# P times V in two row halves of the array: 64-key halves, two PSUM banks, a GpSimd sum, and scores one slot later

## The chip, the cores and the metric

The kernel runs on one core of a Trainium2 chip. The metric is the device time of one execution in microseconds (us). Before the change it is 1067.9 us, the median of three runs (1067.76 to 1069.48).

## What is computed

A block with attention and a gated feed-forward layer side by side, in fp32, on 2048 tokens of width 640:

```python
def _A_ref(x, wqkv, wo):
    H = 32; Dh = D // H; W = 256
    # q, k, v = x @ wqkv, split into 32 heads of 20
    scores = jnp.einsum("bhqd,bhkd->bhqk", q, k) * (Dh ** -0.5)
    mask = (idx[:, None] - idx[None, :] >= 0) & (idx[:, None] - idx[None, :] < W)
    p = _softmax(jnp.where(mask[None, None], scores, -1e9), axis=-1)
    o = jnp.einsum("bhqk,bhkd->bhqd", p, v)
    return o.reshape(B, S, D) @ wo

def _B_ref(x, w_gate, w_up, w_down):
    return (_gelu(x @ w_gate) * (x @ w_up)) @ w_down

xn = _layernorm(A_x)
return A_x + _A_ref(xn, A_wqkv, A_wo) + _B_ref(xn, B_w_gate, B_w_up, B_w_down)
```

What matters here is the window: a query attends to itself and to the 255 keys before it. So a block of 128 keys is seen by 128 + 256 = 384 consecutive queries, and a half block of 64 keys by 64 + 256 = 320.

## The kernel before

The attention is worked off in 32 units `u`: 8 groups `g` of four heads times 4 chunks `c` of 512 queries. A unit is 14 slots long (`NS`), and the loop in `attention()` writes out by hand, slot by slot, the order of TensorE (PE), ScalarE (ACT), VectorE (DVE) and GpSimd (POOL). A slot holds, in this order: the actions that earlier code put off to it (`defer`, `late`, kept by `at` and `tick`), some max work, the scores, and about three (`RATE / NS`) filler matmuls on TensorE (`pull_fill`, line 105): the projections of later heads and part of the feed-forward layer, which would have to be done anyway. After the last unit the rest of the filler runs, and then the remaining feed-forward layer and the output products (lines 901 and 1168).

What is done for a unit, in time order:

- `max_pair` (matmuls on line 473, the reduction on line 477): a first product of scores in bf16 whose row maximum DVE takes. The two heads of a pair stand in the two row halves of the array, each with a PSUM bank of its own from the pool `psm`.
- `exp_piece` (matmuls on line 532, exponential on line 534): the scores again, transposed so that keys lie on the partitions and queries along the free axis, for one head and one of three groups of key blocks X, Z, Y (`pieces`), then ACT writes `exp` into the tile P (`pts[u, bi]`, 128 keys by 4 heads by 512, three buffers). Two pieces are done in each of the even slots 0 to 10. The scores stand in the PSUM pool `psx`, which has two banks.
- `clear` (lines 545 and 548): POOL sets the P entries outside the window to zero, one slot after the last head of a group.
- `av_unit` (line 559), in slot 0 of the next unit: P times V. For each key block of the unit the 128 keys are the contraction, and the four heads stand in four column strips of 32 of the array, with 20 columns of V and a column of ones (the softmax denominator) each. The result of all key blocks is summed in one PSUM bank `ps_o`, from the same pool `psx`. Chunks c > 0 have six key blocks d = -2 to 3 relative to the chunk's first, seen by 128, 256, 384, 384, 256 and 128 of the chunk's 512 queries; chunk 0 has the four blocks d = 0 to 3. ACT then copies the bank to `ob` (line 563), and three slots later `store` issues five DMAs on the SyncE queue (SP): four heads, and the denominators (lines 567 and 568).

P and V are fp32, for which a matmul of the program is executed as two records of a weight load and a matmul: 24 units of 6 blocks and 8 of 4, with 4 heads, are 704 products, and the trace has 1408 records on line 559. Line 105 has single records on hi and lo parts of its operands (fp32r), lines 473 and 532 are bf16.

`load_stack` fetches the scores' operands for unit u + 3 in slots 9 and 12 over SP.

Of the kernel before, what the change touches and what calls it, by code (L numbers as in the profile page):

```python
# [19 lines left out]
C = 512  # L20
# [45 lines left out]
def block_kernel(ctx, tc, x, wqk, wv, wgu, wdo, wdl, out):  # L66
    nc = tc.nc
# [65 lines left out]
    psx = pp.enter_context(tc.tile_pool(name="psx", bufs=2, space=PSUM))  # L133
# [61 lines left out]
    def at(slot, fn, *a):  # L195
        acts.setdefault(slot, []).append((fn, a))
# [9 lines left out]
    def flush():  # L206
        while lates:
            fn, a = lates.pop(0)
            fn(*a)
# [108 lines left out]
    def run(*gens):  # L318
        for gen in gens:
            for _ in gen:  # L320
                pass
# [118 lines left out]
    vtiles = dict(enumerate(v0[2]))  # L440
    ap = pr.enter_context(tc.tile_pool(name="ap", bufs=2, side="right", reuse_waits="tile"))

    def load_stack(u, which=(0, 1)):
        g, c = divmod(u, NC)
        for m in range(80 * g // 128, (80 * g + 79) // 128 + 1):
            assert all((m + 5 * i, c) in done for i in which), (u, m)

        for i in which:
            dst, src, top, again = ((qs[u % NQ], qd[c], 1, 2), (ks[u % NK], kd[c], 0, 0))[i]
            for j in (0, 2):  # L450
                for p, part, n in ((j * 32, top, 2), (j * 32 + 2 * DH, again, 1), (64 - j * 32, 0, 3)):
                    nc.sync.dma_start(dst[p:p + DH * n, j:j + 2].rearrange("p j t -> p (j t)"),
                                      src[g, part:part + n].rearrange("s (d j) t -> (s d) (j t)",
                                                                      j=4)[:, j * C:(j + 2) * C])
# [44 lines left out]
    def pieces(c):  # L499
        b = 4 * c  # L500
        X = [(b, 0, 0, 384)] + ([(b - 2, 384, 0, 128)] if c else [])
        Y = [(b + 1, 0, 128, 384), (b + 3, 384, 384, 128)]
        Z = ([(b - 1, 0, 0, 256)] if c else []) + [(b + 2, 256, 256, 256)]
        return X, Z, Y
# [11 lines left out]
    pts = {}  # L516

    def exp_piece(u, s):
        g, c = divmod(u, NC)
        bi, j = divmod(s, 4)  # L520
        bank = pieces(c)[bi]
        q = qs[u % NQ]
        if j == 0:
            pts[u, bi] = ap.tile([128, 4, C], F32, name="P", tag="P", bufs=3)
        pt = pts[u, bi]
        lo = min(p[1] for p in bank)
        hi = max(p[1] + p[3] for p in bank)
        ps = psx.tile([128, C], F32, name="ps_e", tag="ex")
        for kb, col, q0, n in sorted(bank, key=lambda p: p[3]):
            k = ks[(u - (kb < 4 * c)) % NK]  # L530
            kc = kb % 4 * 128
            nc.tensor.matmul(ps[:, col:col + n], k[0:QROWS, j, kc:kc + 128], q[0:QROWS, j, q0:q0 + n],  # L532
                             start=True, stop=True)
        nc.scalar.activation(pt[:, j, lo:hi], ps[:, lo:hi], AF.Exp, scale=SCALE)  # L534
        if j == 3:
            defer(1, clear, u, bi)
# [13 lines left out]

    def av_unit(u):
        g, c = divmod(u, NC)
        o, v = psx.tile([128, C], F32, name="ps_o", tag="ex"), vtiles[g]
        todo = [(pts[u, bi], *p) for bi, bank in enumerate(pieces(c)) for p in bank]
        for i, (pt, kb, col, q0, n) in enumerate(todo):
            assert (id(v), kb) in done, (u, kb)
            for j in range(4):
                w0_ = kb * 84 + 21 * j
                nc.tensor.matmul(o[32 * j:32 * j + 32, q0:q0 + n], v[:, w0_:w0_ + 32], pt[:, j, col:col + n],  # L559
                                 start=i == 0, stop=i == len(todo) - 1, skip_group_check=True,  # L560
                                 tile_position=(0, 32 * j))
        ob = ap.tile([128, C], F32, name="ob", tag="ob", bufs=1)
        nc.scalar.activation(ob, o, AF.Copy)  # L563

        def store():
            for j in range(4):
                nc.sync.dma_start(od[c].rearrange("(d h) t -> h d t", h=H)[4 * g + j], ob[32 * j:32 * j + DH, :])
            nc.sync.dma_start(sd[c][4 * g:4 * g + 4, :], ob[DH::32, :])

        defer(3, store)  # L570

    def load_gu(f):
        raws = []
# [105 lines left out]
    def x_sums(p, k, half):  # L679
        w = C // 2  # L680
        a, b = (slice((2 * p + i) * C + half * w, (2 * p + i) * C + half * w + w) for i in (0, 1))
        eh, el = xh.bitcast(F32), xl.bitcast(F32)
        live = {}

        def tile_of(i):
            live[i] = ap.tile([128, w], F32, name="tx", tag="tx")
            return live[i]

        def pool(o, i, j, op):
            nc.gpsimd.tensor_tensor(out=o, in0=i, in1=j, op=op)  # L690

        def store(i):
            t = live[i]
            defer(2, lambda: nc.sync.dma_start(td[p][i][:, k, half * w:half * w + w], t))

        def s1():
            pool(tile_of(1), eh[:, k, b], eh[:, k, a], OP.subtract)

        def s2():
            pool(live[1], live[1], el[:, k, b], OP.add)  # L700

        def s3():
# [12 lines left out]

        def s7():
            pool(live[4], live[4], el[:, k + 2, a], OP.add)
            store(4)

        def s8():  # L720
            pool(tile_of(3), eh[:, k + 2, b], eh[:, k, b], OP.subtract)

        def s9():
            pool(live[3], live[3], el[:, k + 2, b], OP.add)

        def s10():
# [28 lines left out]
    def attention():  # L755
        now[0] = -1
        load_stack(0)
        load_stack(1)
        load_stack(2)
        for i, (p, k, half) in enumerate((p, k, half) for p in range(NC // 2) for k in range(2) for half in range(2)):  # L760
            for j, fn in enumerate(x_sums(p, k, half)):
                at(XS0 + XSN * i + 2 * j, fn)
        for i in range(12):
            now[0] = i - 13
            for fn, a in tick():
                fn(*a)
            if i % 2 == 0:
                pull_max(2, now[0])
            flush()
            pull_fill(2 * RAMP)  # L770
        pull_fill(GAP)
        for u in range(NU + 1):
            for i in range(NS):
                T = now[0] = NS * u + i
                for fn, a in tick():
                    fn(*a)
                if i in (0, 4, 8) or T == 2:
                    pull_max(2, T)
                if i == 0 and u:
                    av_unit(u - 1)  # L780
                    flush()
                    pull_max(2, T)
                if i % 2 == 0 and i < 12 and u < NU:
                    exp_piece(u, i)
                    if i == 0 and u:
                        pull_fill(1)
                        debt[0] -= 1
                    exp_piece(u, i + 1)
                flush()
                if u + 3 < NU and i in (KSLOT, 12):  # L790
                    load_stack(u + 3, (int(i == KSLOT),))
                pull_fill(RATE / NS)
        while acts:
            now[0] += 1
            for fn, a in tick():
                fn(*a)
            flush()
        now[0] = None
        run(fill)
        assert not acts  # L800
# [82 lines left out]
    def gate_up_pair(f, w, p, extra, keep=False):  # L883
# [51 lines left out]
        for h, i, g, c in ((h2, qp, g2, 2 * p + 1), (h1, u1, g1, 2 * p)):  # L935
# [3 lines left out]
            else:  # L939
# [4 lines left out]
    place = {("b", 0): "xh1", ("b", 1): "xl1", ("b", 2): "xh0", ("b", 3): "xl0",  # L944
             ("t", 0): "xh2", ("t", 1): "xl2", ("t", 2): "xh3", ("t", 8): "xl3"}
# [433 lines left out]
    for n, (p, k) in enumerate(steps):  # L1379
        i = n % (NQD + 1)  # L1380
# [71 lines left out]
```

## Time and profile before

| | us |
|---|---|
| median of three runs | 1067.9 |
| span of the profiled execution | 1070.0 |
| TensorE busy | 1055.2 |
| VectorE busy | 746.0 |
| ScalarE busy | 518.8 |
| GpSimd busy | 337.8 |
| P times V on TensorE (line 559), 32 units | 84.3 |

The profile is one execution. "PE" is TensorE's matmuls and "PEld" its weight loads, which run beside them. A row of the page's groups reads: line, engine, operation, out<-in, shapes, count, then the busy time and the mean of one, then the idle time of the engine just before it and what ended most of it. A row of the timeline reads: start, length, engine, line, operation, tiles, shape, count; neighbouring instructions of one line are merged into a row, whose shape is that of the first. Ends of matmuls are modelled, so starts are the better guide.

### The profile page before, as it was taken

Reading aid. Unit: us, or ns where it says so; the run is one execution under the profiler, and the core shown is the slowest. Engines: PE = TensorE matmul, PEld = TensorE weight load, DVE = VectorE, ACT = ScalarE, POOL = GpSimd, SP = SyncE. Lnnn points to the kernel's source line nnn. Section 1 sums busy time; section 2 is a strip of 40 time slices with the busy share of each in tenths; the row PEclk is TensorE's granted clock in tenths of the full one; section 3 lists DMA queues with packets and bytes.
Section 4 is the critical chain, followed back from the end, with each engine's and each line's share of the span. In section 5 each row is a group of like instructions: output and inputs, shape, how many; then the busy total and the mean of one; then the engine's idle time right before and its main releaser. Section 6 shows DMA issues by size and latency. Waiting matters only on the chain.

```text
span 1070.0 us, 21147 instructions
## 1 busy us (share of the span) xinstructions
PE 1055.2 (99%) x7253; PEld 830.4 (78%) x7253; DVE 746.0 (70%) x1985; ACT 518.8 (48%) x1088; POOL 337.8 (32%) x514
## 2 busy tenths in 40 slices
PE   8999999999999999999999999999999999999998
PEld 8877666666677766666666668888888999999998
DVE  7845667665565566776767716787776879888887
ACT  4434565566556565565556565332234544433332
POOL 5021564767554383736346340211100000000000
PEclk9999999999999999999999999999999999999999
DMA  5642344446452244424334116576677873443443
GB/s 196 189 131 85 114 135 126 145 131 187 131 153 86 86 120 139 150 85 134 96 116 130 55 60 198 172 245 207 244 247 240 274 261 120 129 131 109 132 132 104
DMA packets 105172, 158.46 MB, mean 148 GB/s; under 512 B 15420, under 2 KB 60092, under 8 KB 105064
## 3 DMA queue, kind: packets, MB, share of 16 engines
q1 hardware_dynamic: 102680, 150.95, 44.5%
q10 hardware_dynamic: 2384, 6.16, 1.8%
q8 instruction: 57, 0.93, 0.4%
q14 instruction: 51, 0.42, 0.1%
HBM read 101.78 MB, written 54.92 MB: 146 GB/s over the span
## 4 chain that ended last, share of the span: by engine, by line
PE 86%; DVE 7%; DMA 2%; ACT 2%; issue 2%; POOL 1%; SPq 0%; ACTq 0%; DVEq 0%; POOLq 0%
PE ps_d L105 27%; PE ps L1168 16%; PE ps_g L901 15%; PE ps_e L532 8%; PE ps_o L559 6%; PE ps_v L105 6%; PE ps_m L473 5%; DVE junk L477 2%; PE ps_g L105 1%; DMA hr<-hd 1%; DVE ss L1006 1%; PE ps_t L180 1%; DVE wt L1006 1%; DVE at L1006 1%; ACT wb L987 1%
## 5 line engine op out<-in xcount | busy, mean ns | idle before, releaser
L477 DVE CUSTOM_DVE_ANT_0 junk<-ps_m,mask 128x384 bf16<-128x384 f32 (+2 forms) x512 | 272.6, 532 | 150.5 <-PE ps_m L473 92.7
L534 ACT ACTIVATE P<-ps_e 128x512 f32<-128x512 f32 (+2 forms) x384 | 198.5, 569 | 93.6 <-PE ps_e L532 79.9
L1168 PE MATMUL ps<-wb,at 128*128 128x320 f32 x999 | 156.7, 309 | 1.1 <-DVE xr L1191 0.7
L1168 PEld LDWEIGHTS ps<-wb,at 128*128 128x128 f32 x999 | 148.9, 188 | 2.1 <-issue 0.9
L545 POOL TENSOR_SCALAR_AFFINE_SELECT P<-P 128x512 f32<-128x512 f32 x128 | 86.1, 672 | 168.0 <-ACT P L534 165.7
L105 PE MATMUL ps_d<-xh,wql 128*128 128x512 f32 x430 | 130.5, 415 | 0.0
L105 PE MATMUL ps_d<-xh,wqh 128*128 128x512 f32 x430 | 129.2, 413 | 0.0
L105 PE MATMUL ps_d<-xl,wqh 128*128 128x512 f32 x430 | 129.2, 412 | 0.0
L532 PE MATMUL ps_e<-qs,ks 124*128 124x128 bf16 (+2 forms) x704 | 117.7, 279 | 0.2 <-ACT ob L563 0.2
L532 PEld LDWEIGHTS <-ks 124*128 124x128 bf16 x704 | 49.6, 98 | 60.5 <-issue 51.1
L105 PEld LDWEIGHTS ps_d<-xl,wqh 128*128 128x128 f32 x430 | 80.1, 191 | 14.8 <-issue 0.8
L105 PEld LDWEIGHTS ps_d<-xh,wql 128*128 128x128 f32 x430 | 80.0, 191 | 13.8
L105 PEld LDWEIGHTS ps_d<-xh,wqh 128*128 128x128 f32 x430 | 79.1, 189 | 15.0 <-ACT xh L188 1.4
L1168 PE MATMUL ps<-wt,at 128*128 128x320 f32 x552 | 89.2, 310 | 0.8 <-DVE xr L1191 0.8
L559 PE MATMUL ps_o<-P,v 128*32 128x384 f32 (+2 forms) x1408 | 84.3, 386 | 0.0
L1168 PEld LDWEIGHTS ps<-wt,at 128*128 128x128 f32 x552 | 82.9, 188 | 1.3 <-DVE xr L1191 1.0
L548 POOL TENSOR_SCALAR_AFFINE_SELECT P<-P 128x512 f32<-128x512 f32 x112 | 72.9, 661 | 28.7 <-ACT P L534 28.7
L1122 ACT ACTIVATE at<-ss 128x512 fp32r<-128x512 f32 x59 | 37.3, 632 | 88.3 <-DVE ss L1006 88.3
L244 POOL TENSOR_TENSOR pt<-r,pt 128x512 bf16<-128x512 f32 x40 | 46.6, 1164 | 90.7 <-ACT pt L243 76.9
L559 PEld LDWEIGHTS ps_o<-P,v 128*32 128x32 f32 x1408 | 41.4, 110 | 39.7 <-issue 25.1
L473 PE MATMUL ps_m<-ks,qs 60*128 60x128 bf16 (+1 forms) x704 | 67.0, 275 | 4.8 <-DVE mx L477 3.1
L563 ACT ACTIVATE ob<-ps_o 128x512 f32<-128x512 f32 x32 | 19.1, 597 | 93.2 <-PE ps_o L559 80.1
(189 smaller groups left out, 1682.4 us busy)
## 6 DMA issues: line engine op xcount, KB each, us to landing
hr<-hd SPq DMA_DIRECT2D x104, 128.0 KB
hd<-he SPq DMA_DIRECT2D x50, 256.0 KB
wr<-wgu SPq DMA_DIRECT2D x27, 320.0 KB
qs<-qd SPq DMA_DIRECT2D x64, 120.0 KB
ks<-kd SPq DMA_DIRECT2D x64, 120.0 KB
xi<-x SPq DMA_DIRECT2D x16, 320.0 KB
qs<-qd SPq DMA_DIRECT2D x64, 80.0 KB
ks<-kd SPq DMA_DIRECT2D x64, 80.0 KB
```

The costliest lines, as they stand in the source:

```text
L105: nc.tensor.matmul(ps, a(k), b(k), start=n == 0, stop=n == 3 * nk - 1)
L244: nc.gpsimd.tensor_tensor(out=pt[:, l, :], in0=r, in1=pt[:, 1, :], op=OP.subtract)
L473: nc.tensor.matmul(ps[:, lo:hi], q[rows, j, 128 * b:128 * b + 128], kt[rows, j, k0:k1], start=True, stop=True, tile_position=(64 * r, 0))
L477: nc.vector.tensor_tensor_reduce(out=junk[:, 0:n], in0=ps[:, 0:n], in1=mask[:, 384 - n:384], scale=1.0, scalar=NEG, op0=OP.add, op1=OP.max ...
L532: nc.tensor.matmul(ps[:, col:col + n], k[0:QROWS, j, kc:kc + 128], q[0:QROWS, j, q0:q0 + n], start=True, stop=True)
L534: nc.scalar.activation(pt[:, j, lo:hi], ps[:, lo:hi], AF.Exp, scale=SCALE)
L545: nc.gpsimd.affine_select(out=a, in_=a, pattern=[[0, 4], [1, 128]], compare_op=OP.is_ge, fill=0.0, base=0, channel_multiplier=-1)
L548: nc.gpsimd.affine_select(out=a, in_=a, pattern=[[0, 4], [-1, 128]], compare_op=OP.is_ge, fill=0.0, base=-1, channel_multiplier=1)
L559: nc.tensor.matmul(o[32 * j:32 * j + 32, q0:q0 + n], v[:, w0_:w0_ + 32], pt[:, j, col:col + n], start=i == 0, stop=i == len(todo) - 1, ski ...
L901: nc.tensor.matmul(ps, i, j, start=first and n == 0, stop=n == len(work) - 1, skip_group_check=True)
L1122: nc.scalar.activation(hi[:, 3:7], s, AF.Copy)
L1168: nc.tensor.matmul(ps[bank][:, 0:HD], *work[bank][j], start=bank not in begun, stop=final[p, bank] == n and j == len(work[bank]) - 1, skip ...
```

## The change

Each key block is taken as two halves r = 0, 1 of 64 keys. The half with r = 0 (partitions 0 to 63 of V and P) stands in the upper row half of the array, the half with r = 1 in the lower one, so a product has 64 rows and 32 columns, at one of eight positions. A half is multiplied with its 320 queries only, cut to the chunk. Each row half sums into a PSUM bank of its own, both from `psx`. The order of the halves is written out (`steps_`): six pairs, one of each row half, with 320, 256, 192, 320, 128 and 64 queries for c > 0; in chunk 0 the halves that belong to blocks before the sequence are left out.

ACT copies the first bank to `ob` and the second to a part of the P tile of group Y, which is read no more (`oc`). Three slots later POOL adds the two (`join`), and the store is put off from three slots to five. The scores' pieces stand in the odd slots 1 to 11 in place of the even ones, with the same two pieces in each.

```diff
     def av_unit(u):
         g, c = divmod(u, NC)
-        o, v = psx.tile([128, C], F32, name="ps_o", tag="ex"), vtiles[g]
-        todo = [(pts[u, bi], *p) for bi, bank in enumerate(pieces(c)) for p in bank]
-        for i, (pt, kb, col, q0, n) in enumerate(todo):
+        v = vtiles[g]
+        os = [psx.tile([128, C], F32, name="ps_o", tag="ex") for _ in range(2)]
+        place = {kb - 4 * c: (pts[u, bi], col, q0) for bi, bank in enumerate(pieces(c)) for kb, col, q0, n in bank}
+
+        def half(d, r):
+            i = 2 * d + r
+            return d, r, max(0, 64 * i), min(C, 64 * i + 320)
+
+        steps_ = [((0, 0), (0, 1)), ((2, 0), (-1, 1)), ((-1, 0), (2, 1)), ((1, 0), (1, 1)),
+                  ((3, 0), (-2, 1)), ((-2, 0), (3, 1))]
+        todo = [half(*x) for pair in steps_ for x in pair if x[0] in place]
+        begun_, left = set(), [sum(t[1] == r for t in todo) for r in range(2)]
+        for d, r, qa, qb in todo:
+            pt, col, q0 = place[d]
+            kb = 4 * c + d
...
+            rows = slice(64 * r, 64 * r + 64)
             for j in range(4):
                 w0_ = kb * 84 + 21 * j
-                nc.tensor.matmul(o[32 * j:32 * j + 32, q0:q0 + n], v[:, w0_:w0_ + 32], pt[:, j, col:col + n],
-                                 start=i == 0, stop=i == len(todo) - 1, skip_group_check=True,
-                                 tile_position=(0, 32 * j))
-        ob = ap.tile([128, C], F32, name="ob", tag="ob", bufs=1)
-        nc.scalar.activation(ob, o, AF.Copy)
+                nc.tensor.matmul(os[r][32 * j:32 * j + 32, qa:qb], v[rows, w0_:w0_ + 32],
+                                 pt[rows, j, col + qa - q0:col + qb - q0], start=r not in begun_,
+                                 stop=not left[r], skip_group_check=True, tile_position=(64 * r, 32 * j))
+            begun_.add(r)
+        ob, oc = ap.tile([128, C], F32, name="ob", tag="ob", bufs=1), pts[u, 2][:, 0]
+        lo = 0 if c else 64
+        nc.scalar.activation(ob, os[0], AF.Copy)
+        nc.scalar.activation(oc[:, lo:], os[1][:, lo:], AF.Copy)
+
+        def join():
+            nc.gpsimd.tensor_tensor(out=ob[:, lo:], in0=ob[:, lo:], in1=oc[:, lo:], op=OP.add)
...
-        defer(3, store)
+        defer(3, join)
+        defer(5, store)
...
-                if i % 2 == 0 and i < 12 and u < NU:
-                    exp_piece(u, i)
-                    if i == 0 and u:
+                if i % 2 and i < 12 and u < NU:
+                    exp_piece(u, i - 1)
+                    if i == 1 and u:
                         pull_fill(1)
                         debt[0] -= 1
-                    exp_piece(u, i + 1)
+                    exp_piece(u, i)
```

More of the change, by code (lines that the diff above doesn't have):

```diff
@@ L552, in av_unit @@
         g, c = divmod(u, NC)
-        o, v = psx.tile([128, C], F32, name="ps_o", tag="ex"), vtiles[g]
-        todo = [(pts[u, bi], *p) for bi, bank in enumerate(pieces(c)) for p in bank]
-        for i, (pt, kb, col, q0, n) in enumerate(todo):
+        v = vtiles[g]
[11 more added lines that the diff above has]
+            kb = 4 * c + d
             assert (id(v), kb) in done, (u, kb)
+            left[r] -= 1
+            rows = slice(64 * r, 64 * r + 64)
             for j in range(4):
                 w0_ = kb * 84 + 21 * j
-                nc.tensor.matmul(o[32 * j:32 * j + 32, q0:q0 + n], v[:, w0_:w0_ + 32], pt[:, j, col:col + n],
-                                 start=i == 0, stop=i == len(todo) - 1, skip_group_check=True,
-                                 tile_position=(0, 32 * j))
-        ob = ap.tile([128, C], F32, name="ob", tag="ob", bufs=1)
-        nc.scalar.activation(ob, o, AF.Copy)
+                nc.tensor.matmul(os[r][32 * j:32 * j + 32, qa:qb], v[rows, w0_:w0_ + 32],
[8 more added lines that the diff above has]
+            nc.gpsimd.tensor_tensor(out=ob[:, lo:], in0=ob[:, lo:], in1=oc[:, lo:], op=OP.add)
         def store():
```

## The prediction

> **What bounds the kernel now.** I read the page's busy times and slices first, then the chain that ended last, then busy times by stage, and last who waited for whom.
>
> ```profile
> span 1070.0 us, 21147 instructions
> PE 1055.2 (99%) x7253; PEld 830.4 (78%) x7253; DVE 746.0 (70%) x1985; ACT 518.8 (48%) x1088; POOL 337.8 (32%) x514
> PE   8999999999999999999999999999999999999998
> PE 86%; DVE 7%; DMA 2%; ACT 2%; issue 2%; POOL 1%; SPq 0%; ACTq 0%; DVEq 0%; POOLq 0%
> ```
> ```profile
> 110.00:640.00 530.00, 526.80 (x4163) 351.65 (x4166) 333.07 (x1104) 308.19 (x654) 287.69 (x454) 1.00 0.40 119
> ```
> ```profile
> PE ps_m L473 <- DVE mx L477: 3.1, 9, 0.5
> PE ps_e L532 <- ACT ob L563: 0.2, 1, 0.2
> ```
>
> In the stage with attention (110 to 640 us; columns PE, PEld, DVE, ACT, POOL, granted clock, DMA share, GB/s) TensorE is busy for 526.8 of 530 us at full clock, the others at most 333. TensorE's waits there are 3.1 us for the row maxima and 0.2 for the copy of P times V. So what a matmul costs is paid in full, and work on the others is free as long as nobody on TensorE waits for it. The filler is a fixed amount: time saved in a unit ends the stage earlier.
>
> P times V, by unit: two calls of the windows view restricted to line 559, one over the 8 units of chunk 0 and one over the 24 others; the first row and the sum of each.
>
> ```profile
> 110.30:113.60 3.30, 2.15 (x32) 0.94 (x32) 1.00 0.00 0
> sum 26.40, PE 17.17 PEld 7.46; mean PE 2.15 PEld 0.93
> ```
> ```profile
> 127.30:130.60 3.30, 2.80 (x48) 1.42 (x48) 1.00 0.49 147
> sum 79.20, PE 67.14 PEld 33.98; mean PE 2.80 PEld 1.42
> ```
>
> Chunk 0 streams 384 + 384 + 256 + 128 = 1152 queries per head, the others 1536. Then 67.14 / 24 - 17.17 / 8 = 0.651 us for 384 queries: **1.70 ns per query**, all four heads and both records together.
>
> How the array is shared shows in one unit's timeline.
>
> ```profile
> 400.57 1.30 PE L105 MATMUL ps_d<-xh,wqh 128*128 128x512 f32 x5
> 401.70 0.84 PE L105 MATMUL ps_d<-xh,wql 128*128 128x512 f32 x3
> 401.95 0.63 POOL L545 TENSOR_SCALAR_AFFINE_SELECT P<-P 128x512 f32<-128x512 f32 x1
> 402.91 0.16 PEld L559 LDWEIGHTS ps_o<-P,v 128*32 128x32 f32 x8 [0.16 <-issue]
> 402.91 2.80 PE L559 MATMUL ps_o<-P,v 128*32 128x384 f32 x48
> 403.26 0.13 PEld L559 LDWEIGHTS ps_o<-P,v 128*32 128x32 f32 x4 [0.19 <-issue]
> 403.58 1.21 PEld L559 LDWEIGHTS ps_o<-P,v 128*32 128x32 f32 x28 [0.19 <-issue]
> ...
> 405.64 0.50 PE L473 MATMUL ps_m<-ks,qs 60*128 60x384 bf16 x4
> 405.78 0.60 ACT L563 ACTIVATE ob<-ps_o 128x512 f32<-128x512 f32 x1 [2.37 <-DMA qs<-qd]
> 406.07 0.39 PE L532 MATMUL ps_e<-qs,ks 124*128 124x128 bf16 x2
> ```
>
> A plain matmul of 512 columns takes (401.70 - 400.57) / 5 = 0.226 us, 0.44 ns per column. The weight loads of P times V come in fours, 403.58 - 403.26 = 0.32 us apart for 384 queries: 0.84 ns per query for a round of four records, about twice a plain pass. So a round is the four column strips at work together, and a block is two rounds. Two row halves work together too, in line 473: four matmuls of 384 columns take 406.07 - 405.64 = 0.43 us with the switch at their end, where one after the other they would take 4 x 384 x 0.44 ns = 0.68 us. No row shows four strips and two row halves at once, and that is what the change stands on.
>
> **The change, part by part.**
>
> *Fewer queries per array position.* A row half streams 320 + 256 + 192 + 320 + 128 + 64 = 1280 queries in place of 1536; in chunk 0, 1024 (upper) and 896 (lower) in place of 1152. If all eight positions work at once, a unit saves 256 x 1.70 ns = 0.435 us, in chunk 0 128 x 1.70 = 0.217 us: 24 x 0.435 + 8 x 0.217 = **-12.2 us**. Its bounds are the rivals below: from this to a sum in which the halves do not overlap.
>
> *Twice the weight loads and matmuls*: 1408 more of each.
>
> ```profile
> L559 PEld LDWEIGHTS ps_o<-P,v x1408: 105/110/110, 110.4 to 640.3; 128*32 128x32 f32 x176
> L559 PE MATMUL ps_o<-P,v x1408: 272/379/511, 110.4 to 640.4; 128*32 128x384 f32 x64, 128*32 128x256 f32 x56, 128*32 128x128 f32 x56
> L559 PEldq EVENT_SEMAPHORE  x31: 51/51/51, 107.8 to 636.0; - x31
> ```
>
> A load (0.110 us) runs behind the round before it. A round of 64 queries lasts 64 x 0.84 = 0.054 us, so the last two of a unit can each be 0.056 us late: at most 32 x 0.112 = +3.6 us, at best 0, since loads and matmuls start together at 402.91. I take +1.0, nearer that row.
> Feeding them: eight loads start within 0.16 - 0.11 = 0.05 us at 402.91, 6 ns each, and the sequencer passes the first unit's semaphore at 107.8, 2.6 us ahead of the first matmul (110.4). So I cost it at nothing; the upper bound is the pace of line 473, 0.43 us for four records, 0.11 us each, and is a rival.
> The Trainium skill ("TensorE: Matmul & The Clock Gate", "Wait — 56ns, not 53.3ns?") gives a floor of about 25 ns from start to start. By it 96 matmuls would take at least 2.4 us, an estimate, a unit would save 0.2 us in place of 0.435, and the time would come out near 1063; the 6 ns above disagree for different array positions.
>
> *A second bank, a second copy.* Both banks of `psx` are taken by P times V, whose first matmul so waits for both last exponentials; these lie two slots back. After it ACT makes two copies. Before, the copy starts 405.78 - 405.64 = 0.14 us after the next matmul and takes 0.60; so `ob` is done 0.74 and `oc` at most 1.34 us after that matmul. In the built order four of line 473 (0.43) and three of line 105 (0.68) come before the first scores: 1.11 us. One more of line 105 and the first scores (512 columns each, 0.45) come before the second: 1.56 us. Both are covered, the second by 0.2 us. Without the filler the second scores would wait 1.34 - 0.43 - 0.23 = 0.68 us, 32 x 0.68 = +22 us. I take +0.5. ACT's 32 x 0.60 = 19 us lie in 530 - 308 us of room.
>
> *The sum on POOL.*
>
> ```profile
> L244 POOL TENSOR_TENSOR pt<-r,pt 128x512 bf16<-128x512 f32 x40 | 46.6, 1164 | 90.7 <-ACT pt L243 76.9
> L545 POOL TENSOR_SCALAR_AFFINE_SELECT P<-P 128x512 f32<-128x512 f32 x128 | 86.1, 672 | 168.0 <-ACT P L534 165.7
> ```
> ```profile
> L559 PE MATMUL ps_o<-P,v 128*32 128x384 f32 (+2 forms) x1408 | 84.3, 386 | 0.0
> ```
> ```profile
>   PEld ps_o L559: 2.0, 11
> ```
>
> An add of this size takes 1.164 us (line 244): 32 x 1.164 = 37 us on POOL, 288 + 37 = 325 of 530. It stands in slot 3, when both copies have long landed. Behind it on POOL are the clears of the new unit's X, not read before the next P times V ten slots on, and the lo parts of filler weights. Cost 0. The five store DMAs move two slots back on SP, behind other stores but ahead of the loads of slot 9, which serve three units later; `ob` is written again 14 slots on. Cost 0.
>
> *Scores one slot later.* In the built order three fewer matmuls of line 105 lie between the last scores and P times V: the last clear ends 0.68 us later, at 402.58 + 0.68 = 403.26 in this unit, 0.35 us after the start at 402.91. Group Y is first needed after 320 + 256 + 192 queries, 1.30 us in. Line 545 lists 2.0 us in 11 waits of weight loads for POOL; the matmuls of line 559 have no idle time before them. I take +0.3; a unit in four late by 0.4 us would be +3.
>
> Sum on the profiled time: 1070.0 - 12.2 + 1.0 + 0.5 + 0.3 = 1059.6. The median of the runs lies 2.1 us below the span: **1057.5 us, rounded to 1057**.
>
> **The rivals.**
>
> *A: order is kept between the row halves of a strip.* The program issues, for each half, a head's two records one behind the other. If the lower half's first record does not pass the upper half's second, only neighbours overlap. Rounds of a unit are then 320, then each pair's own length (1280 in sum), the larger of neighbouring pairs (320 + 256 + 320 + 320 + 128), and 64: 3008 queries at 0.85 ns, against 2 x 1536 = 3072. That is -0.054 us per unit, in chunk 0 2368 against 2304 or +0.054: -0.9 us in all, +1.8 from above: 1070.9 on the profiled time, 1068.8 on the median. For it: line 473 alternates halves with one record each, so no row shows a passing. Against it: in the strips the four heads do work together although each has two records to do.
> The Trainium skill (same page, Part 3, "The mechanism") says that matmuls start and end in strict program order. By that rule this rival is what happens; the loads in fours agree with it only if the order is not head by head.
>
> *B, the other side: the array takes four streams at a time.* Place: the 24 + 8 blocks of line 559. Price: the halves run one after the other, 2560 queries against 1536 and in chunk 0 1920 against 1152: 24 x 1024 x 1.70 ns + 8 x 768 x 1.70 = 41.8 + 10.4 = +52 us, 1120 on the median. It decides as soon as rounds hold four records instead of eight (break-even is at 4 x 2560 / 1536 = 6.7). For it: every round in the trace has four. Against it: line 473 reads two row halves at once, and the data per partition and time are the same as before.
>
> *C: feeding binds.* At 0.11 us per record 96 take 10.6 us; at half that, with the queue filled ahead, 5.3 us: (5.3 - 2.8) x 24 + (3.5 - 2.15) x 8 = +71, 1139. Against it: the lead of 2.6 us.
>
> *D: a new wait.* The cover after P times V is too short because ACT comes late to the copies, and half of the 22 us above is paid: 1057 + 11 = 1068; all of it, 1079.
>
> **How the numbers follow.** Forecast 0.55, A 0.17, B 0.10, C 0.05, D 0.13. About 0.2% (2.1 us) is what a measurement of this kernel can tell from no change. Faster takes the forecast and a sliver of D: 0.56. Same takes most of A and a part of D: 0.16. Slower is B, C, the rest of D and a bit of A: 0.28. The forecast's own range is 1055 (no cost at all, 1067.9 - 12.2) to 1063 (3.6 for loads, 3 for clears). To hold 8 in 10 it is carried over A and D to 1079, with 1054 below; B and C are left out.
>
> **What would show each step.** Forecast: loads of P times V in eights, a unit of about 2.37 us busy (chunk 0: 1.94), line 559's successor at about 72 us in all, and still about 0 idle before the scores. A: 2.75 us per unit, loads in fours. B: 4.5 us. C: rounds further apart than 0.84 ns per query, with "issue" as what ended the gaps. D: idle time of the scores' matmuls with the copies as releaser, or of P times V with POOL. The forecast is wrong if the unit does not shrink, or if it does and TensorE's idle time in the stage grows by more than 4 us.

## The result and the profile after

| | before | after |
|---|---|---|
| median of the runs, us | 1068.69 (4 runs, 1067.76 to 1070.49) | 1077.11 (4 runs, 1075.19 to 1078.79) |
| span of the profiled execution, us | 1070.0 | 1073.8 |
| P times V on TensorE, us | 84.3 | 76.2 |

The changed kernel is slower by 0.75%: ratio 1.0075, 95% interval 1.0056 to 1.0094. Forecast were 1057 us and "faster"; 1077 lies inside the stated range only because that range was carried over rivals A and D, and neither of them came true. Part of the scatter of the runs goes with the granted clock of a run: those of before that were taken with experiments 1 to 4 took 1066.0 to 1068.2 us at 1.0 and 1070.9 to 1071.7 at 0.995. From the profile's page of the changed kernel, the busy times and the chain:

```profile
span 1073.8 us, 24088 instructions
...
PE 1056.4 (98%) x8661; PEld 824.3 (77%) x8661; DVE 753.1 (70%) x1985; ACT 531.4 (49%) x1120; POOL 373.8 (35%) x546
...
PE 81%; DVE 6%; DMA 4%; POOL 3%; issue 3%; ACT 2%; SPq 1%; ACTq 0%; DVEq 0%; POOLq 0%
```

TensorE still is the bound. But it is busy for 1.2 us more than before although P times V takes 8.1 us less. The groups by line, for P times V and for the filler:

```profile
L105 PE MATMUL ps_d<-xh,wql 128*128 128x512 f32 x430 | 136.8, 421 | 0.0
L573 PE MATMUL ps_o<-P,v 64*32 64x320 f32 (+4 forms) x2816 | 76.2, 348 | 2.5 <-ACT P L534 1.8 <-POOL P L548 0.5
L105 PEld LDWEIGHTS ps_d<-xl,wqh 128*128 128x128 f32 x430 | 77.4, 189 | 18.6 <-issue 7.6
L105 PEld LDWEIGHTS ps_d<-xh,wql 128*128 128x128 f32 x430 | 77.0, 189 | 20.7 <-issue 10.2
L105 PEld LDWEIGHTS ps_d<-xh,wqh 128*128 128x128 f32 x430 | 76.7, 189 | 21.1 <-issue 8.9 <-ACT xh L188 1.4 <-DVE he L648 0.3
```

The same groups before:

```profile
L105 PE MATMUL ps_d<-xh,wql 128*128 128x512 f32 x430 | 130.5, 415 | 0.0
L105 PEld LDWEIGHTS ps_d<-xl,wqh 128*128 128x128 f32 x430 | 80.1, 191 | 14.8 <-issue 0.8
L105 PEld LDWEIGHTS ps_d<-xh,wql 128*128 128x128 f32 x430 | 80.0, 191 | 13.8
```

Two things stand out. The filler, in which not one instruction was changed, got dearer: 136.8 for 130.5 us in one of its three groups. And its weight loads now stand idle for 7 to 10 us per group with "issue" as the releaser, where it was 0.8 or nothing. "Issue" names no tile; the timeline has to say where it is. P times V has idle time of its own, 2.5 us, mostly on the last exponentials.

To see where the stage gained and lost, every TensorE matmul between the first and the last P times V was charged from its own start to the start of the next, and the times were added by kind of work. "Places" counts how often TensorE comes into the filler from maximum work or from the small matmul that transposes the maxima (line 494), and not from scores. Times in us:

```
                    places  filler  PxV   max   scores  stage
before                   0   337.4  82.2  55.4    53.2  530.0
after                  118   349.3  74.8  58.2    54.0  537.2
```

The stage is 7.2 us longer, P times V 7.4 shorter, the filler 11.9 longer. (Starts also shift what is charged to whom, so the stage is the firm number.) The span grew by 3.8 us only: in the profiled execution of after the stage began at 107.67 us, before at 110.41. The windows view shows a difference that accounts for it: ahead of the stage the granted clock (third number from the end) was 0.97 in before and 1.00 in after, and 3% of 110 us are 3.3 us. First before, then after:

```profile
0.00:110.00 110.00, 103.75 (x653) 88.41 (x655) 70.01 (x211) 46.88 (x141) 31.20 (x48) 0.97 0.47 150
0.00:110.00 110.00, 103.06 (x726) 86.42 (x727) 71.82 (x218) 47.21 (x142) 31.25 (x48) 1.00 0.46 150
```

Experiment 1 below, whose program up to the stage is that of after, had 0.97 there and began the stage at 110.60. In the stage the clock was 1.00 in all of them. The medians differ by 8.4 us.

TensorE's timeline in the unit that the prediction shows. First P times V and what follows it, after:

```profile
405.12 2.45 PE L573 MATMUL ps_o<-P,v 64*32 64x320 f32 x96
407.50 0.63 PE L473 MATMUL ps_m<-ks,qs 60*128 60x384 bf16 x4
408.06 0.73 PE L105 MATMUL ps_d<-xh,wql 128*128 128x512 f32 x2
408.62 0.40 PE L105 MATMUL ps_d<-xl,wqh 128*128 128x512 f32 x1
408.86 0.40 PE L532 MATMUL ps_e<-qs,ks 124*128 124x128 bf16 x2
408.96 0.53 PE L105 MATMUL ps_d<-xl,wqh 128*128 128x512 f32 x1
409.33 0.40 PE L532 MATMUL ps_e<-qs,ks 124*128 124x128 bf16 x2
```

Before, the rows that follow those in the prediction:

```profile
406.17 0.53 PE L105 MATMUL ps_d<-xh,wql 128*128 128x512 f32 x1
406.54 0.40 PE L532 MATMUL ps_e<-qs,ks 124*128 124x128 bf16 x2
```

P times V now goes from 405.12 to 407.50, 2.38 us in place of 405.64 - 402.91 = 2.73. Behind the maximum work, before, came a piece of scores and one filler matmul, 1024 columns in 406.54 - 406.07 = 0.47 us. After come two filler matmuls, also 1024 columns, and take 408.62 - 408.06 = 0.56 us. A piece of scores with one filler matmul still takes 409.33 - 408.86 = 0.47 in after. So 0.09 us is lost where the maximum work is followed by filler. The weight loads at these places, after and then before:

```profile
408.05 0.30 PEld L105 LDWEIGHTS ps_d<-xh,wql 128*128 128x128 f32 x2 [0.45 <-issue]
408.39 0.19 PEld L105 LDWEIGHTS ps_d<-xl,wqh 128*128 128x128 f32 x1
...
408.93 0.19 PEld L105 LDWEIGHTS ps_d<-xl,wqh 128*128 128x128 f32 x1
```
```profile
406.07 0.11 PEld L532 LDWEIGHTS <-ks 124*128 124x128 bf16 x2 [0.32 <-issue]
406.14 0.19 PEld L105 LDWEIGHTS ps_d<-xh,wql 128*128 128x128 f32 x1
```

Either way the weight loader stands still until the maximum work is over (0.45, 0.32 us, "issue"; the 0.13 more in after is a matmul of the maximum work that came late, see the section on why the prediction was wrong). What it loads then can't be hidden. After, that is a filler weight, long (0.19 us) and needed at once; a second load follows 0.109 us behind (starts 408.053 and 408.162). Before, it was a short scores weight, and the filler's load at 406.14 ran behind the scores at 406.07. That is the "issue" in the filler's rows.

### The profile page after: what moved, and what is told of

It is laid out like the page before. It is cut to its first block, busy times and chain, and to the rows that moved or that the text cites. A ratio compares the mean times of both kernels' runs of the same rounds, so it can differ in the third digit from the quotient of the medians.

```text
span 1073.8 us, 24088 instructions
## 1 busy us (share of the span) xinstructions
PE 1056.4 (98%) x8661; PEld 824.3 (77%) x8661; DVE 753.1 (70%) x1985; ACT 531.4 (49%) x1120; POOL 373.8 (35%) x546
## 4 chain that ended last, share of the span: by engine, by line
PE 81%; DVE 6%; DMA 4%; POOL 3%; issue 3%; ACT 2%; SPq 1%; ACTq 0%; DVEq 0%; POOLq 0%
PE ps_d L105 25%; PE ps L1189 16%; PE ps_g L922 15%; PE ps_e L532 7%; PE ps_v L105 6%; PE ps_o L573 6%; PE ps_m L473 4%; PE ps_g L105 1%; DVE junk L477 1%; POOL pt L244 1%; DVE at L1027 1%; DVE ss L1027 1%; DMA kd<-pt 1%; POOL wql L614 1%; PE ps_t L180 1%
## 5 line engine op out<-in xcount | busy, mean ns | idle before, releaser
L105 PE MATMUL ps_d<-xh,wql 128*128 128x512 f32 x430 | 136.8, 421 | 0.0
L105 PE MATMUL ps_d<-xh,wqh 128*128 128x512 f32 x430 | 135.3, 420 | 0.0
L105 PE MATMUL ps_d<-xl,wqh 128*128 128x512 f32 x430 | 134.8, 418 | 0.0
L545 POOL TENSOR_SCALAR_AFFINE_SELECT P<-P 128x512 f32<-128x512 f32 x128 | 82.5, 644 | 106.9 <-ACT P L534 106.6
L105 PEld LDWEIGHTS ps_d<-xh,wql 128*128 128x128 f32 x430 | 77.0, 189 | 20.7 <-issue 10.2
L105 PEld LDWEIGHTS ps_d<-xh,wqh 128*128 128x128 f32 x430 | 76.7, 189 | 21.1 <-issue 8.9
L105 PEld LDWEIGHTS ps_d<-xl,wqh 128*128 128x128 f32 x430 | 77.4, 189 | 18.6 <-issue 7.6
L548 POOL TENSOR_SCALAR_AFFINE_SELECT P<-P 128x512 f32<-128x512 f32 x112 | 70.9, 643 | 35.8 <-ACT P L534 35.8
L573 PE MATMUL ps_o<-P,v 64*32 64x320 f32 (+4 forms) x2816 | 76.2, 348 | 2.5 <-ACT P L534 1.8
L573 PEld LDWEIGHTS ps_o<-P,v 64*32 64x32 f32 x2816 | 48.5, 106 | 29.8 <-issue 5.6
```

What stands on the lines that cost most here:

```text
L105: nc.tensor.matmul(ps, a(k), b(k), start=n == 0, stop=n == 3 * nk - 1)
L545: nc.gpsimd.affine_select(out=a, in_=a, pattern=[[0, 4], [1, 128]], compare_op=OP.is_ge, fill=0.0, base=0, channel_multiplier=-1)
L548: nc.gpsimd.affine_select(out=a, in_=a, pattern=[[0, 4], [-1, 128]], compare_op=OP.is_ge, fill=0.0, base=-1, channel_multiplier=1)
L573: nc.tensor.matmul(os[r][32 * j:32 * j + 32, qa:qb], v[rows, w0_:w0_ + 32], pt[rows, j, col + qa - q0:col + qb - q0], start=r not in begun ...
```

## The experiments

The theories at first: **E**, scores moved by a slot pull apart what stood together, TensorE comes into the filler more often, and each such entry costs; **F**, the new form of P times V slows the filler behind it; **G**, the sum on GpSimd delays something. Later **H**: late scores cost as such, whatever TensorE does at which place.

**1. The shift alone.** Before, with the scores in the odd slots:

```diff
-                if i % 2 == 0 and i < 12 and u < NU:
-                    exp_piece(u, i)
-                    if i == 0 and u:
+                if i % 2 and i < 12 and u < NU:
+                    exp_piece(u, i - 1)
+                    if i == 1 and u:
                         pull_fill(1)
                         debt[0] -= 1
-                    exp_piece(u, i + 1)
+                    exp_piece(u, i)
```

> The kernel before with nothing changed but the slots of the scores (odd instead of even); P times V as before. In the program the filler of line 105 is then entered from another kind of matmul 336 times in the attention stage instead of 217. Theory E (each entry into the filler costs about 0.10 us): filler 337 to 349 us in the stage, with 2.8 us more for the maxima about +14 us, 1083 (1079 to 1085). Rival F (twice as many instructions of P times V slow what follows them on TensorE): no change, 1067 to 1071. Rival G (the sum on GpSimd makes everything late): no change, 1067 to 1071.

Measured: 1078.79 us, ratio 1.0095 (1.0071 to 1.0119); stage 539.1, filler 349.0. That is just under the range expected for E, and far from F and G. From the groups by line:

```profile
L105 PE MATMUL ps_d<-xh,wql 128*128 128x512 f32 x430 | 137.6, 423 | 0.0
L559 PE MATMUL ps_o<-P,v 128*32 128x384 f32 (+2 forms) x1408 | 84.6, 386 | 0.5 <-POOL P L548 0.4
L105 PEld LDWEIGHTS ps_d<-xh,wql 128*128 128x128 f32 x430 | 77.7, 191 | 20.0 <-issue 9.2
```

The filler is as dear as in the whole change, with the same "issue", and P times V is the old one. F and G can't explain it. A step that was costed at +0.3 us loses as much as the whole change (stage +9.1 us).

**2. The change without the shift.** The new P times V, scores in the even slots:

> The change without its last part: P times V in two row halves, two copies and the GpSimd sum, but scores in the even slots as before. Theory E: 217 entries as before, filler back at 337 us (within 3); P times V 24 x 0.35 + 8 x 0.22 = 10.2 us shorter where it does not stall; but the first two score pieces of a unit stand right behind it and wait for the copies, about 0.35 and 0.2 us, 15 us in all: 1073 (1068 to 1077). Rival F: filler stays near 349 us, 1080 or more. Rival G: P times V still loses some 5 us to late GpSimd work in units 1 to 11; not told apart from E by the total.

Measured: 1071.64 us, 1.0021 (1.0006 to 1.0036); stage 530.6, filler 338.3, P times V 73.8. The filler is back, but the gain isn't there. TensorE's timeline behind P times V:

```profile
405.12 0.63 PE L473 MATMUL ps_m<-ks,qs 60*128 60x384 bf16 x4
405.85 0.38 PE L532 MATMUL ps_e<-qs,ks 124*128 124x128 bf16 x2
```

And the waits of TensorE for ACT there (sum, times, longest):

```profile
PE ps_e L532 <- ACT ob L579: 1.8, 6, 0.7
```

The first scores come 0.73 us after the maximum work's start, not 0.43. By 0.13 us the fourth matmul of the maximum work is late (405.432, for VectorE, see below); the rest, 0.17, is theirs: they need a bank of `psx`, and both hold P times V until ACT's copies. Behind P times V the maximum work is charged with 28.7 us (before 20.0). So the shift had a use: it hides the copies. Half of the answer is that the change takes two banks from the scores, and the other half is what it does to get them back.

**3. Only the first pair late** (pairs in slots 1, 2, 4, 6, 8, 10):

```diff
-                if i % 2 and i < 12 and u < NU:
-                    exp_piece(u, i - 1)
-                    if i == 1 and u:
+                s = {1: 0, 2: 2, 4: 4, 6: 6, 8: 8, 10: 10}.get(i)
+                if s is not None and u < NU:
+                    exp_piece(u, s)
+                    if s == 0 and u:
                         pull_fill(1)
                         debt[0] -= 1
-                    exp_piece(u, i)
+                    exp_piece(u, s + 1)
```

> The change, but only the first two score pieces of a unit are one slot later (slot 1); the other ten stay in even slots 2 to 10. 248 entries into the filler. Theory E: +31 x 0.10 = +3 us for entries, -10.2 us for P times V, 0 to 5 us of stalls on GpSimd: 1062 to 1067, faster than before. Rival F: the filler stays at 349 us, 1072 to 1077. Rival G: units 1 to 11 lose 5 us and more, 1066 to 1070, with the filler at 337 to 341 us.

Measured: 1073.04 us, 1.0047 (1.0031 to 1.0062), a miss; stage 533.7. The filler fell to 340.5 as expected, but scores took 58.3 (before 53.2), and the 5 us more lie in the pieces of slot 2 (14.2 for 9.2): four pieces within two slots, which share two banks. The maximum work behind P times V took 24.7 us (before 20.0). P times V was 72.9 us, the least of all: with the last scores in slot 10 again, it was too long in one unit (unit 9, 0.9 us) and nowhere late to start.

**4. More entries from scores.** Before, with one filler matmul between the two pieces in all even slots, not only slot 0; TensorE enters the filler 372 times for 217:

```diff
-                    if i == 0 and u:
+                    if u:
                         pull_fill(1)
```

> The kernel before with one filler matmul between the two score pieces in every even slot instead of only in slot 0; all else as before. 372 entries into the filler instead of 217. Theory E: +155 x 0.10 = +15.5 us, 1084 (1079 to 1088), all of it in the filler's time of the stage. Rivals F and G: no change, 1067 to 1071.

Measured: 1072.02 us, 1.0037 (1.0022 to 1.0052), a miss that changed the theory. 155 more entries made the stage 531.7 - 530.0 = 1.7 us longer, about 0.01 us each (by the medians 3.3 / 155 = 0.02). An entry as such costs next to nothing. What remained is **E2**: only an entry that doesn't come from scores costs, about 0.1 us. The "places" of the table above are such entries.

**5. The maximum work moved along.** The change, and the maximum work of slots 4 and 8 (with the transposing matmul) one slot later too, so that it stands ahead of scores again:

```diff
-MXD = 6
+MXD = 7
...
-                if i in (0, 4, 8) or T == 2:
+                if i in (0, 5, 9) or T == 3:
```

> The change, with the max work of slots 4 and 8 moved along to slots 5 and 9, so that scores stand right behind it again, and the negated maxima's transposition one slot later too. Of the 119 places where filler follows the row-half matmuls of the maxima or that transposition instead of scores, 88 are gone. Theory E2 (leaving the row-half mode for filler exposes the filler's weight load, about 0.107 us, where scores expose 0.012): 58 to 88 times 0.095 us = 5.5 to 8 us less than the change, 1069 to 1072. Rival H (the scores themselves are late, whatever stands before them): as the change, 1076 to 1078.

Measured: 1068.41 us, 0.9995 (0.9984 to 1.0007), 8.7 us less than the change, a little more than expected; stage 528.6 (537.2 - 8.6), filler 340.3. The scores are as late as in the change. H falls.

**6. The same with the old P times V**: experiment 1 with this edit.

> The kernel with scores shifted and P times V as before (the first experiment), with the max work of slots 4 and 8 moved along to slots 5 and 9. Theory E2: 5.5 to 8 us less than the shift alone (1078.8), 1070 to 1073. Rival H: as the shift alone, 1078 to 1080.

Measured: 1070.58 us, 1.0013 (0.9998 to 1.0028); stage 530.3, 8.8 us less than in experiment 1. 5 and 6 each remove 88 of the places (58 behind maximum work, 30 behind the transposing matmul): 8.6 / 88 and 8.8 / 88 are **0.10 us per place**, the same with both forms of P times V.

**7. The sum on VectorE**, in experiment 5's kernel:

```diff
-            nc.gpsimd.tensor_tensor(out=ob[:, lo:], in0=ob[:, lo:], in1=oc[:, lo:], op=OP.add)
+            nc.vector.tensor_tensor(out=ob[:, lo:], in0=ob[:, lo:], in1=oc[:, lo:], op=OP.add)
...
-        defer(3, join)
+        defer(3, late, join)
```

> The change with the max work moved along (as the kernel above it) and the sum of the two halves on VectorE instead of GpSimd, in the same slot. If GpSimd's extra 37 us make the early units late (P times V there lost 4.7 us beyond its 2.38 and 1.86 us per unit), they go: 3 to 5 us less than with the sum on GpSimd, 1065 to 1068. If not, the same as with the sum on GpSimd, or up to 2 us more from VectorE's 32 x 0.7 us.

Measured: 1067.14 us, 0.9982 (0.9963 to 1.0); the median lies in the range expected if GpSimd made units late, but the intervals of 5 and 7 overlap, and the stage is 528.8. P times V still has 75.0 us and the same late units. So G falls for these too, and the sum on GpSimd costs nothing that these runs can tell.

**8. Places without a shift.** Before, with the maximum work of slots 4 and 8 behind the scores of the same slot; 217 entries as ever, 58 of them from maximum work:

```diff
-                if i in (0, 4, 8) or T == 2:
+                if i == 0 or T == 2:
                     pull_max(2, T)
...
                     exp_piece(u, i + 1)
+                if i in (4, 8):
+                    pull_max(2, T)
```

> The kernel before, with the max work of slots 4 and 8 put behind the scores of the same slot instead of ahead of them; nothing else is changed. 58 times filler instead of scores follows the row-half matmuls. Theory E2: 58 x 0.095 = +5.5 us, 1074 (1072 to 1077). Rival H and a theory by which only the number of entries into the filler counts (it stays 217): no change, 1067 to 1070.

Measured: 1074.2 us, 1.0062 (1.0039 to 1.0086); stage 534.5, + 4.5 / 58 = 0.08 us per place. Neither the shift nor P times V is in this kernel: two statements exchanged cost 0.6%.

**9. Other banks for P times V.** The change, with scores in the even slots, P times V in two of `psm`'s four banks, and the maximum work spread so that these are free:

```diff
-        os = [psx.tile([128, C], F32, name="ps_o", tag="ex") for _ in range(2)]
+        os = [psm.tile([128, C], F32, name="ps_o", tag="mx") for _ in range(2)]
...
-                if i in (0, 4, 8) or T == 2:
+                if i in (2, 6, 10):
                     pull_max(2, T)
-                if i == 0 and u:
-                    av_unit(u - 1)
-                    flush()
-                    pull_max(2, T)
+                if i == 0:
+                    pull_max(1, T)
+                    if u:
+                        av_unit(u - 1)
+                        flush()
+                    pull_max(1, T)
...
```

> The changed kernel with three edits: P times V sums in two banks of psm, the four-bank pool of the maximum work, instead of the two banks of psx; the scores go back to the even slots; and the eight maximum items of a unit are spread as 1 before and 1 after P times V, then 2 each ahead of the scores of slots 2, 6 and 10. So nothing lies between the maximum work and the scores, and the scores' banks are free after P times V. Places where TensorE comes into the filler: 217, as before the change. Theory (it is the way out of the row-half mode straight into the filler that costs, and late scores that make P times V late): P times V saves its nominal 24 x 0.352 + 8 x 0.216 = 10.2 us with no excess in units 1 to 11 beyond 2 us; one more place of maximum work per unit costs at most 31 x 0.12 = 3.7 us; filler within 2 us of 337; median 1061 to 1065, against 1068.7 before. Rival I (the two-bank form of P times V needs its cover, whatever the pool: the wait moves from the scores to the maximum work of slot 0 or 2): maximum work or scores grow by 8 us or more and the median stays at 1068 to 1073. Rival J (what makes P times V late in units 1 to 11 is its own order of the halves, not the slot of the scores): P times V in units 1, 2, 6, 7, 8, 10 and 11 is again 0.2 to 0.8 us too long each, about 4 to 5 us, median 1066 to 1069.

Measured: **1061.13 us, 0.9912 (0.989 to 0.9934)**, faster than both kernels. The page and TensorE's timeline around P times V:

```profile
span 1060.4 us, 24082 instructions
```
```profile
397.68 0.34 PE L473 MATMUL ps_m<-ks,qs 60*128 60x128 bf16 x4
397.95 2.45 PE L573 MATMUL ps_o<-P,v 64*32 64x320 f32 x96
400.32 0.34 PE L473 MATMUL ps_m<-ks,qs 60*128 60x128 bf16 x4
400.60 0.39 PE L532 MATMUL ps_e<-qs,ks 124*128 124x128 bf16 x2
```

Scores follow the maximum work at once and find their banks free. Rivals I and J fall: maximum work and scores were charged 53.8 and 53.1 us, no more than before, and P times V was too long by 1.6 us in all, 1.2 of it in unit 9 alone. The filler, 339.5, is half a us above what was expected. At the same granted clock (0.995) its runs took 1060.9 to 1062.2 us, those of before alongside 1071.55 to 1072.68, about 10 us more, so the 8.2 us between the medians is rather too little. The new spread of the maximum work was not run with the old P times V, so its share isn't measured by itself; by the charges P times V is 8.7 us shorter than before, the maximum work 1.6, and the filler 2.1 longer. The same table for all kernels (in 4 and 8 the filler's column can't be compared: the time of a piece of scores is in part charged to the filler behind it, and how often that happens was changed; there the stage tells):

```
                    places  filler  PxV   max   scores  stage  median
before                   0   337.4  82.2  55.4    53.2  530.0
after                  118   349.3  74.8  58.2    54.0  537.2  1077.11
1 shift alone          118   349.0  82.8  52.7    53.7  539.1  1078.79
2 no shift               0   338.3  73.8  64.1    52.5  530.6  1071.64
3 first pair late       30   340.5  72.9  60.1    58.3  533.7  1073.04
4 more entries           0   354.6  82.2  55.7    37.3  531.7  1072.02
5 maximum along         30   340.3  75.1  57.8    53.5  528.6  1068.41
6 the same, old PxV     30   339.9  82.9  52.5    53.2  530.3  1070.58
7 sum on VectorE        30   340.0  75.0  58.4    53.6  528.8  1067.14
8 maximum behind        58   330.7  82.2  55.0    64.8  534.5  1074.20
9 other banks            0   339.5  73.5  53.8    53.1  521.8  1061.13
```

## Why the prediction was wrong

**The step that failed is "Scores one slot later", taken at +0.3 us.** It asked only who comes late to P times V, the clears. It did not ask what stands beside the scores on TensorE once they are gone. Maximum work stands in slots 0, 4 and 8, the transposing matmul in slot 6; scores stood directly behind all of them, and in odd slots filler does. 118 places at 0.1 us are 11.8 us. Experiment 1 shows the step alone: 539.1 - 530.0 = +9.1 us, in which the maximum work behind P times V came out 2.8 us cheaper (17.2 for 20.0). The order of the instructions, which the prediction used to count cover, had this in it.

**Its other half, the late clears, was a mechanism that is there, with too small a size and one part missing.** In the unit shown the last clear was forecast to end 0.35 us after the start of P times V, and that did no harm there. Other units did not have that margin. Unit 7 of after, ACT and then PE and POOL in the timeline:

```profile
230.50 0.60 ACT L262 ACTIVATE pt<-ps_d 128x512 bf16<-128x512 f32 x1 [2.57 <-DMA kd<-pt]
230.99 0.73 ACT L609 ACTIVATE wqh<-wr 128x640 fp32r<-128x640 f32 x1
231.61 1.08 ACT L534 ACTIVATE P<-ps_e 128x512 f32<-128x512 f32 x2
```
```profile
232.35 2.91 PE L573 MATMUL ps_o<-P,v 64*32 64x320 f32 x96 [1.49 <-ACT P L534]
...
234.00 0.64 POOL L545 TENSOR_SCALAR_AFFINE_SELECT P<-P 128x512 f32<-128x512 f32 x1
```

ACT waits 2.57 us for the store of an old `pt`, whose buffer it needs, and the last two exponentials stand behind that on ACT. P times V starts late, and then waits for the clears, the last of which begins at 234.00. Before, ACT had such a wait too, at the same point of the program, but the unit's last exponentials stood ahead of it:

```profile
226.18 1.09 ACT L534 ACTIVATE P<-ps_e 128x512 f32<-128x512 f32 x2 [0.24 <-PE ps_e L532]
227.84 0.60 ACT L262 ACTIVATE pt<-ps_d 128x512 bf16<-128x512 f32 x1 [0.57 <-DMA kd<-pt]
```

Over all units P times V of after lasts 2.8 us longer than its regular 2.378 (chunk 0: 1.863) and starts 1.9 us late, 4.7 together, nearly all in units 1 to 11; +3 was the bound. Over the whole stage its weight loads are listed with 8.5 us of waiting for the clears, where before and experiment 9 have 3.0 (experiment 1 has 8.0 too, but there P times V came out only 0.7 us too long):

```profile
PEld ps_o L573 <- POOL P L548: 4.9, 18, 1.0
PEld ps_o L573 <- POOL P L545: 3.6, 9, 0.4
```

The loss takes both parts of the change: 0.8 us with late scores and the old P times V (experiment 1), 1.8 with the new one and early scores (2), 1.0 with only the first pair late (3), 5.0 in 5. Why the two together cost more than each was not followed unit by unit, and stays open.

**P times V itself was right.** The unit went from 2.730 to 2.378 us (chunk 0: 2.079 to 1.863): 24 x 0.352 + 8 x 0.216 = -10.2 us, where -12.2 and +1.0 for weight loads were put. All eight array positions work at once. Starts of the 96 matmuls of the unit at 405.12, by rounds of eight, in ns:

```
queries   320  320  256  256  192  192  320  320  128  128   64   64
first       0  293  562  778  994 1156 1319 1588 1857 1966 2076 2139
eighth     46  340  609  825 1041 1203 1366 1635 1904 2013 2136 2230
```

A round of 320 takes 269 ns, one of 128 takes 109: 0.84 ns per query as before, with eight records in it and not four. Rival A (rounds of four between the halves), rival B (four streams) and C (feeding) fall. The missing us is at the ends: the first round is 24 ns longer than the others of its size, and the last two of 64 queries take 63 and over 91 ns where 54 were due, so in the last round the records themselves set the pace, some 13 ns each ((2230 - 2139) / 7). That is the weight loads' term: +2.0 where +1.0 was taken, within its bounds.

On the rules of the Trainium skill that the prediction weighed ("TensorE: Matmul & The Clock Gate"): by the floor of about 25 ns from start to start ("Wait — 56ns, not 53.3ns?") a round of eight could not take 109 ns, as it does here; across array positions the measurement decides against it. The strict program order between matmuls of the Trainium skill (same page, Part 3, "The mechanism") would have given rival A if the two records of a head are in the program one behind the other; rounds of eight speak against that.

**Part of the gain went to a wait that no step named: VectorE's maxima.** The prediction shows this wait in its rows (3.1 us in 9 waits before) and has no term for it. The maximum work behind P times V needs banks whose maxima VectorE must have read. Those ran behind P times V; a shorter P times V uncovers them. VectorE in after, in the unit above, and then in experiment 1 with the old P times V (its maximum work starts at 409.52):

```profile
407.19 0.56 DVE L477 CUSTOM_DVE_ANT_0 junk<-ps_m,mask 128x384 bf16<-128x384 f32 x1
407.67 0.08 DVE L477 DVE_READ_ACCUMULATOR2_ANT mx<- 128x1 f32 x1
```
```profile
408.86 0.56 DVE L477 CUSTOM_DVE_ANT_0 junk<-ps_m,mask 128x384 bf16<-128x384 f32 x1
409.34 0.08 DVE L477 DVE_READ_ACCUMULATOR2_ANT mx<- 128x1 f32 x1
```

In after VectorE is done at 407.75, 0.25 us behind the start of the maximum work (407.50); its fourth matmul starts at 407.81. In experiment 1 it is done at 409.42, in time. From its start to the next work the maximum work takes 0.56 us where it took 0.43 in chunks 1 and 3 (chunk 0: 1.08 for 0.86; chunk 2 keeps its 0.43), so chunk 0 gives its whole 0.216 us back there. Without units 8 to 10, which wait for other reasons, it is 18.5 us for 15.0: +3.5. In those three it waits 2.5 us less, which leaves +1.0.

The terms close: -10.2 (P times V) + 4.7 (late) + 1.0 (maxima) + 118 x 0.1 = +7.3 us, for 7.2 measured in the stage of the two profiled executions.

**The other terms.** Cover of the copies, +0.5: right. ACT's copies in after:

```profile
407.57 0.60 ACT L579 ACTIVATE ob<-ps_o 128x512 f32<-128x512 f32 x1 [2.04 <-DMA qs<-qd]
408.07 0.59 ACT L580 ACTIVATE P<-ps_o 128x512 f32<-128x512 f32 x1
```

The second is done at 408.66, 0.2 us before the first scores (408.86), and TensorE has no listed wait for either. Without the cover 22 us were forecast, and experiment 2 measured 8.7, with what the maxima take of it: in the unit shown the copy makes the first scores 0.17 us late, and behind them the second scores come after the usual 0.48 us, so the second copy costs nothing more. Rival D, too short a cover, did not happen. The sum on POOL, 0: right; it takes 40.1 us there, for 37. The stores were not tried apart.

The chance of 0.56 for faster rested on a list of costs in which three waits of TensorE had no line: the filler's load behind the maximum work, the exponentials behind an ACT stall, and the maxima under P times V.

## What to carry to other kernels

Before a step is moved in an order written by hand, look at the pairs of neighbours on the bounding engine that the move makes and breaks, not only at who now comes late: two kinds of work that follow each other cheaply may each be dear beside a third, and exchanging two statements was worth 4.5 us here. A change that shortens a stretch of the bounding engine also shortens the cover of all that ran behind it; ask for each of these whether it still fits. And where a change needs buffers, ask which pool can spare them: with both banks of the scores' two, the new P times V came out between 2.4 us less (experiment 7) and 8.4 us more than before, by what was done to cover the copies; with two of the maxima's four, and the maximum work spread for it, 8.2 us less.

## What the runs showed of the hardware

- The cost of an entry into the filler depends on what stands ahead of it: 0.01 to 0.02 us behind scores (experiment 4), 0.08 behind maximum work (8), 0.10 behind maximum work and the transposing matmul taken together (5 and 6). Behind maximum work, which stands in two row halves, the weight loader started only when that work was over (idle 0.45 us, before 0.32), while it loads alongside a plain matmul (a filler load at 408.393, beside the matmul started at 408.390). What is lost fits one load: the next load started 0.109 us behind the first and the second filler matmul 0.104 us late (0.335 us behind the first, for 0.231). The Trainium skill ("TensorE: Matmul & The Clock Gate", "LDWEIGHTS (loading the stationary operand)") gives columns / 1.2, an estimate of 107 ns for these 128; the distance of the two loads in the trace agrees, the lengths that the profile lists don't (0.19 us for these 128 columns, 0.11 us for the 32 of P times V). Why the loader waits there was not tried by itself, and row halves are not needed for it: at the one place where filler stands directly behind the old P times V (experiment 1, at 634.55), which uses all rows in four column strips, the second filler matmul came 0.341 us behind the first as well.
- Behind the transposing matmul, which uses all rows, the filler's load did start alongside (431.331, both), but a matmul of 128 columns is too short to hide it: the second filler matmul came 0.313 us behind the first.
- Eight matmuls of 64 rows by 32 columns run together as fast as four of 128 by 32: 0.84 ns per query for a round of either.
